# Moving the second part of a modulation weight from SyncE's DMA queue to ACT's in the prologue of a transformer block

## The chip, the cores and the metric

The kernel runs on one core of one Trainium2 chip. The metric is the device time in microseconds (us), the median of several executions of the whole program. One execution of each kernel is profiled; its trace has a span, from the first to the last instruction, some 1.8 us shorter than the device time.

## The reference, cut to what matters

The block is attention with 32 query heads over cached keys and values, followed by a gated MLP with a spatial matmul. Both halves are preceded by a layer norm whose result is scaled and shifted by values computed from a small vector c:

```python
mod = (_silu(c) @ w_mod).reshape(c.shape[0], 6, 1, -1)
sa, ca, ga, sb, cb, gb = (mod[:, 0], mod[:, 1], ...)      # cut
h = _layernorm(x, axis=-1) * (1 + ca) + sa
x = x + ga * _A_ref(h, A_k_cache, A_v_cache, A_wq, A_wo)
```

w_mod is 512 x 3072 in bf16. Only its first two column blocks of 512 (for sa and ca) are needed before the first queries can be projected. The kernel calls them part 0 and part 1, of 512 KB each.

## The kernel before

The order in which loads are issued (cuts marked with ...):

```python
nc.scalar.dma_start(out=c_bf[:], in_=c_dram)
nc.scalar.dma_start(out=x_sb[:, 0, :], in_=x_dram[:, 0, :])
for i in range(2):
    part = slice(i * D, (i + 1) * D)
    nc.sync.dma_start(out=wmod_a[:, :, part], in_=wmod_dram[:, :, part])
...
wqs[0] = early.tile([P, NDT, REP * DH], BF16, name="wq_g")
for dts in (slice(0, 2), slice(2, 4)):
    nc.sync.dma_start(out=wqs[0][:, dts, :], in_=wq_dram[:, dts, 0 : REP * DH])
load_k_nat(0)
nc.sync.dma_start(out=x_sb[:, 1, :], in_=x_dram[:, 1, :])
load_k_nat(1)
...   # further x tiles, the rest of the keys, values, output weights
```

What TensorE does with them. warm(n) issues n matmuls on zeros whose result nobody reads; they bridge the time until data is there and keep the clock up:

```python
xns0 = ln1_norm(0, 1, ln1_stats(0, 1))     # x tile 0, on DVE and GpSimd
mc_ps = bank("misc")
warm(10)
mod_part(0, wmod_a, 0, mc_ps)              # 16 small matmuls, need part 0: "product 1"
warm(6)
mod_part(1, wmod_a, D, mc_ps)              # 16 small matmuls, need part 1: "product 2"
...                                        # transposes of xn, modc, hT, query projection,
                                           # then scores (PE) and exponentials (ACT)
```

## Time and profile before

| | before |
|---|---|
| device time, median (3 runs) | 1321.19 us |
| device time, median (6 runs: these 3 and 3 more, beside the changed kernel) | 1321.04 us (1320.58 to 1321.67) |
| span of the profiled execution (its device time was 1321.45 us, 0.4 above the median) | 1319.7 us |
| product 1 starts, product 2 starts | 5.42, 7.81 us |
| first exponential of the attention starts (ACT) | 11.49 us |

The lines that carry the argument stand in the prediction below. Two more are used: how the loads are issued, and when the first exponential starts. They are from the timelines of SyncE and of ACT; the columns are start in us, duration in us, engine, source line, operation, tiles and count.

```profile
0.73 1.36 SPq L701 DMA_DIRECT2D wmod_a<-in_w_mod_dram  x2
2.13 1.13 SPq L746 DMA_DIRECT2D wq_g<-in_A_wq_dram  x2
11.49 5.61 ACT L980 ACTIVATE pT<-s_ps 128x1024 bf16<-128x1024 f32 x6 [0.68 <-PE s_ps L973]
```

SPq is SyncE's issuing: both parts of the modulation weight first, then the query weights wq_g (512 KB in two halves). The third line begins the attention. From there TensorE and ACT run as a chain to the end.

### The profile page before, as it was taken

The page shows a single profiled execution, that of the slowest core. Times are in us where ns is not written, and L with a number is a line of the kernel's source. Part 1 is how long each engine was busy: PE and PEld are TensorE (multiplying, and loading weights), DVE is VectorE, ACT ScalarE, POOL GpSimd, SP SyncE. Part 2 cuts the span into 40 slices and gives each one's busy share as a digit, 9 for nine tenths or more (in the row PEclk, how much of TensorE's full clock was granted, in tenths as well). Part 3 has the DMA queues.
Part 4 walks back from the last instruction along what each step waited for, and adds up shares of the span by engine and source line. Part 5 has one row for each costly group of instructions (what it writes and reads, how often), then busy time and mean ns, then how long its engine had stood idle before and what let it go on. Part 6 is the DMA issues. An engine that isn't in the chain of part 4 may idle for free.

```text
span 1319.7 us, 27930 instructions
## 1 busy us (share of the span) xinstructions
PE 1312.4 (99%) x12359; PEld 858.6 (65%) x12359; DVE 470.7 (36%) x1162; ACT 1077.1 (82%) x1061; POOL 51.4 (4%) x96
## 2 busy tenths in 40 slices
PE   9999999999999999999999999999999999999998
PEld 5666666666666666666666666666666666644445
DVE  5622222222222222222222222222222566794444
ACT  7899999999999999999999999999999999650000
POOL 1201000000000000000000000000000000020000
PEclk9999999999999999999999999999999999999999
DMA  6542121112101111211110211121111112144300
GB/s 180 146 99 46 21 45 37 37 17 50 37 17 37 30 37 37 33 33 38 33 38 13 53 38 33 17 53 22 33 13 21 25 31 32 34 114 81 70 20 26
DMA packets 148944, 58.64 MB, mean 44 GB/s; under 512 B 138480, under 2 KB 144880, under 8 KB 148816
## 3 DMA queue, kind: packets, MB, share of 16 engines
q1 hardware_dynamic: 141792, 37.65, 15.4%
q0 software_dynamic: 4432, 16.91, 4.5%
q10 hardware_dynamic: 2592, 2.23, 0.5%
q8 instruction: 98, 1.61, 0.5%
q14 instruction: 30, 0.25, 0.1%
HBM read 21.89 MB, written 2.10 MB: 18 GB/s over the span
## 4 chain that ended last, share of the span: by engine, by line
PE 99%; DVE 0%; ACT 0%; issue 0%; DVEq 0%
PE o_ps L995 35%; PE s_ps L973 33%; PE misc L1027 8%; PE misc L940 8%; PE misc L1336 7%; PE s_ps L1182 2%; PE s_ps L1221 2%; PE o_ps L1357 1%; PE o_ps L781 1%; PE s_ps L1357 1%; PE misc L850 0%; DVE hT L809 0%; PE misc L1344 0%; ACT pT L980 0%; DVE tmp L1369 0%; DVE yout L1370 0%
## 5 line engine op out<-in xcount | busy, mean ns | idle before, releaser
L980 ACT ACTIVATE pT<-s_ps 128x1024 bf16<-128x1024 f32 x1024 | 1043.8, 1024 | 82.0 <-PE s_ps L973 6.7
L995 PEld LDWEIGHTS <-pT 128*128 128x128 bf16 x8192 | 548.5, 98 | 241.2
L995 PE MATMUL o_ps<-v,pT 128*128 128x129 bf16 x8192 | 631.5, 220 | 0.0
L973 PE MATMUL s_ps<-qT,kT 128*128 128x512 bf16 x2048 | 608.9, 379 | 0.3 <-ACT pT L980 0.2
L1006 DVE RECIPROCAL rall<-o_ps 128x2 f32<-128x2 f32 x256 | 43.5, 170 | 744.5 <-PE o_ps L995 741.1
L973 PEld LDWEIGHTS <-kT 128*128 128x128 bf16 x2048 | 199.3, 98 | 119.2 <-issue 0.8
L1027 PE MATMUL misc<-wo_g,oT 128*128 128x512 bf16 x512 | 194.1, 379 | 0.0
L940 PE MATMUL misc<-hT,wq_g 128*128 128x512 bf16 (+2 forms) x528 | 190.7, 371 | 0.1
L1007 DVE TENSOR_TENSOR onorm<-o_ps,rall 128x256 bf16<-128x256 f32 x256 | 108.6, 424 | 8.8
L1336 PE MATMUL misc<-wsp,z 128*128 128x512 bf16 (+2 forms) x560 | 100.7, 336 | 0.0
L951 DVE CAST qT<-misc 128x512 bf16<-128x512 f32 x127 | 86.2, 679 | 2.0 <-PE misc L940 2.0
L1336 PEld LDWEIGHTS <-z 128*128 128x128 bf16 x560 | 50.6, 98 | 48.5
L1040 DVE TENSOR_TENSOR xacc<-misc,xacc 128x512 f32<-128x512 f32 x112 | 76.0, 678 | 0.0
L940 PEld LDWEIGHTS <-wq_g 128*128 128x128 bf16 x528 | 50.4, 98 | 1.2 <-issue 0.4
L1027 PEld LDWEIGHTS <-oT 128*128 128x128 bf16 x512 | 50.1, 98 | 0.8
L1351 DVE TENSOR_TENSOR gb<-misc,bsp_bc 128x512 bf16<-128x512 f32 (+1 forms) x28 | 18.4, 658 | 58.9 <-PE misc L1336 58.9
L1182 PE MATMUL s_ps<-win_sb,hT 128*128 128x448 bf16 x128 | 27.0, 352 | 0.0
L1192 ACT ACTIVATE z<-s_ps 128x896 bf16<-128x896 f32 x16 | 14.7, 917 | 14.9 <-PE s_ps L1182 14.9
L1221 PE MATMUL s_ps<-hT,win_sb 128*128 128x512 bf16 x112 | 24.5, 379 | 0.0
L1229 ACT ACTIVATE z1T<-s_ps 128x1024 bf16<-128x1024 f32 x14 | 14.3, 1023 | 10.1 <-PE s_ps L1221 9.1
L692 DVE BATCH_NORM_STATS2 bnst<-x_sb 128x6 f32<-128x512 bf16 x32 | 21.8, 683 | 1.3 <-DMA x_sb<-in_A_x_dram 0.8
L1357 PE MATMUL o_ps<-wout_sb,yT 128*128 128x512 bf16 x84 | 20.1, 379 | 0.0
(88 smaller groups left out, 269.6 us busy)
## 6 DMA issues: line engine op xcount, KB each, us to landing
wq_g<-in_A_wq_dram POOLq DMA_DIRECT2D x7, 512.0 KB, 3.8
v<-in_A_v_cache_dram POOLq DMA_DIRECT2D x7, 512.0 KB, 6.0
wo_g<-in_A_wo_dram POOLq DMA_DIRECT2D x7, 512.0 KB, 4.7
oT<-onorm SPq DMA_TRANSPOSE x128, 2.4
wsp<-in_w_mod_dram POOLq DMA_DIRECT2D x1, 2048.0 KB, 9.0
out_dram<-yout ACTq DMA_DIRECT2D x16, 128.0 KB, 1.7
win_sb<-in_B_w_in_dram POOLq DMA_DIRECT2D x1, 1792.0 KB, 7.8
x_sb<-in_A_x_dram SPq DMA_DIRECT2D x3, 512.0 KB, 5.6
```

The costliest lines, as they stand in the source:

```text
L940: nc.tensor.matmul(ps[0][:, o0 : o0 + n], lhsT=wqs[g][:, dt, hh * DH : (hh + 1) * DH], rhs=hTs[ch][:, dt, c0 : c0 + n], start=(dt == 0), s ...
L951: nc.vector.tensor_copy(out=dst, in_=src)
L973: nc.tensor.matmul(s_ps[:, h * 512 : (h + 1) * 512].rearrange("p (r q) -> p r q", r=REP), lhsT=groups[g]["kT"][:, kt * P : (kt + 1) * P], ...
L980: nc.scalar.activation(out=pTs[u][:, 2 * i : 2 * i + 2, :], in_=s_ps[:].rearrange("p (k q) -> p k q", k=2), func=ACT.Exp, scale=inv_sqrt_dh,)
L995: nc.tensor.matmul(o_ps[:, hh % 2, 0 : DH + 1], lhsT=pTs[u][:, kt, hh * P : (hh + 1) * P], rhs=groups[g]["v1"][:, kt, 0 : DH + 1], start=( ...
L1007: nc.vector.tensor_tensor(out=onorms[u][:, hh - 1 : hh + 1, :], in0=o_ps[:, :, 0:DH], in1=rall[:, c0 : c0 + 2].unsqueeze(2).to_broadcast([ ...
L1027: nc.tensor.matmul(X_ps[:], lhsT=oTs[u][:, hh, :], rhs=groups[g]["wo"][:, hh, :], start=(hh == 0), stop=(hh == REP - 1),)
L1040: nc.vector.tensor_tensor(out=xaccs[j][:], in0=X_ps[:], in1=xaccs[j][:], op=ALU.add)
L1182: nc.tensor.matmul(ps[0][:, hf * 512 : hf * 512 + FC], lhsT=h2Ts[j // CT][:, dt, (j % CT) * P : (j % CT + 1) * P], rhs=win_sb[:, dt, FH + ...
L1221: nc.tensor.matmul(ps[0][:, k * 512 : (k + 1) * 512], lhsT=win_sb[:, dt, f * P : (f + 1) * P], rhs=h2Ts[2 * ch2 + k][:, dt, :], start=(dt ...
L1336: nc.tensor.matmul(g_ps[:, :n], lhsT=z2[:, st, f * P : (f + 1) * P], rhs=wsp[t][:, st, c0 : c0 + n], start=(st == 0), stop=(st == NT - 1 a ...
L1357: nc.tensor.matmul(dst, lhsT=yT[:, f, jj * P : (jj + 1) * P], rhs=wout_sb[:, f, :], start=(f == 0), stop=(f == NFT - 1),)
```

## The change

The intent: take one issue off SyncE, bring part 1 in by the queue that is idle after x tile 0, and let the query weights come right behind part 0.

```diff
     for i in range(2):
         part = slice(i * D, (i + 1) * D)
-        nc.sync.dma_start(out=wmod_a[:, :, part], in_=wmod_dram[:, :, part])
+        (nc.sync, nc.scalar)[i].dma_start(
+            out=wmod_a[:, :, part], in_=wmod_dram[:, :, part]
+        )
```

Nothing else is edited.

## The prediction

> **What bounds the kernel now.** I read the page first, then the chain of waits, then the first 12 us of the timeline, and last the DMA queues in short windows. The page says that TensorE (PE) is the bound from end to end: it is busy in every slice, and the chain that ended last runs over it.
>
> ```profile
> span 1319.7 us, 27930 instructions
> PE 1312.4 (99%) x12359; PEld 858.6 (65%) x12359; DVE 470.7 (36%) x1162; ACT 1077.1 (82%) x1061; POOL 51.4 (4%) x96
> PE 99%; DVE 0%; ACT 0%; issue 0%; DVEq 0%
> ```
>
> The three loads that the change touches are all issued in the first 4 us, and what they feed is over by 10.3 us. So at most 10 of 1320 us (0.8%) are in play at all, and a verdict outside 2% is out of reach by arithmetic. What remains is how far the start shifts, because what follows is a chain without slack: a later start is a later end by the same amount. The chain in order of time, cut to the prologue:
>
> ```profile
> 1.18 4.45 PE o_ps L781 x10
> 5.62 0.41 PE misc L850 x16
> 6.03 1.95 PE o_ps L781 x6
> 7.98 0.39 PE misc L850 x16
> ...
> 8.39 0.16 DVE modc L860
> 8.55 0.08 DVE modc L861
> ...
> 8.73 0.35 DVE hT L809
> ```
>
> L781 are warm-up matmuls whose result nobody reads. L850 are the two modulation products: the first 16 need part 0 of the modulation weight, the second 16 part 1. After them come the modulation columns, hT, the query projection and the first scores. No DMA stands in this chain, but one is just under it. In the list of waits, PE's only wait for a load before 11 us is this:
>
> ```profile
> PEld L850 <- DMA wmod_a<-in_w_mod_dram: 0.5, 1, 0.5
> ```
>
> and the timeline shows that it costs almost nothing today:
>
> ```profile
> 4.14 1.49 PE L781 MATMUL o_ps<-onorm 128*128 128x512 bf16 x3
> 5.24 0.70 PEld L850 LDWEIGHTS <-wmod_a 128*128 128x128 bf16 x16 [0.52 <-DMA wmod_a<-in_w_mod_dram]
> 5.42 0.61 PE L850 MATMUL misc<-sc_bf,wmod_a 128*128 128x1 bf16 x16
> 7.60 0.66 PEld L850 LDWEIGHTS <-wmod_a 128*128 128x128 bf16 x16
> ```
>
> The weight-load side waited 0.52 us, until part 0 landed at 5.24; but the tenth warm-up matmul still streamed. The warm-ups start every 0.43 us from 1.18, so the tenth starts near 5.03 and streams until about 5.45, and the first product starts at 5.42. Part 0 lands exactly when PE becomes free: its slack is nil, and each delay of it is a delay of PE. Part 1 has slack: issued at 1.47 and landed 5.6 us later, near 7.1, against 7.60 where PE takes it.
>
> **What the Trainium skill says.** "DMA: Bandwidth & Descriptors", section "Issuing engines are not separate DMA queues", says that loads issued from SyncE and ACT run on the same 16 engines and interleave, and that a second issuer only saves sequencer time. The same page, section "Queues, rings and completion order", says that SyncE and ACT own one queue row each, and that each DMA engine goes round-robin between the rows with work, packet by packet. The trace agrees: between 3.6 and 3.8 us, while ACT's queue carried x tile 0 and SyncE's carried part 0, the windows show 34 packets of the one and 30 of the other. "TensorE: Matmul & The Clock Gate", section "Part 1: The HAM clock gate", says that PE runs at half rate until it was busy through a free-running window of some 3.4 us. The trace shows warm-up matmuls 0.43 us apart until about 7.17 and some 0.22 apart from there, so the release came about 6.0 us after the first matmul. "ScalarE: Activation LUTs", section "What ACT_TABLE_LOAD costs", gives some 1283 ns; this trace has 1.28 us.
>
> **Part 1: SyncE loses one issue.** The two issues took 1.36 us together, 0.61 to 0.70 each. Everything behind on SyncE is issued some 0.65 us earlier: the query weights at about 1.45 and not 2.13. That gains nothing, since from about 3.6 us on the DMA engines are full and the order of bytes decides. The query weights, issued at 2.13 and 2.83 and 5.7 us in landing, are there at 7.8 and 8.5; their first weight load is at 8.65, behind hT, and its wait is on "issue" and not on a DMA. With the bytes ahead of them doubled up with part 1, they land at about the same time. The key tiles behind them follow the same total of bytes. Value: 0.
>
> **Part 2: ACT gets one issue, 0.6 to 0.7 us.** Its issues end at 1.59 now, the table load runs from 1.62 to 2.90, the exponential from 2.91, and the last small operation of that string (sc_bf on DVE) ends at 3.93. All of it shifts by 0.65 to about 4.6. DVE's next work is at 4.69 (the statistics of x tile 0), and PE needs sc_bf at 5.42. It fits. Value: 0, with 0.1 us to spare on DVE and over a microsecond behind that before xn (ready at 7.03, used at 8.22).
>
> **Part 3: part 1 now competes with part 0.** In one queue part 1 waited behind part 0. In ACT's queue it stands only behind x tile 0, which finishes first. The queue counts from the start of the span, to 4.4, 4.8 and 6.2 us:
>
> ```profile
> q1 hardware_dynamic: 415, 0.42, 29.8%
> q10 hardware_dynamic: 288, 0.13, 12.0%
> ...
> q1 hardware_dynamic: 575, 0.57, 36.9%
> ...
> q1 hardware_dynamic: 1061, 1.06, 51.4%
> ```
>
> q10 is ACT's queue; it stands at its final 288 packets by 4.4 (the same short windows put the last x packets at 4.3). A part is 512 packets of 1 KB and 16 small ones at the end: 528. The windows give q1 351 at 4.2, 494 at 4.6 and 575 at 4.8, so part 0 is through at 4.6 + 0.2 x 34/81 = 4.68, and landed 0.55 later. With part 1 ready in q10 from 4.3 on, q1 gets about half of some 78 packets per 0.2 us: its remaining 528 - 351 = 177 packets from 4.2 on take 177/39 x 0.2 = 0.91 us, until 5.11. Delay of part 0: 5.11 - 4.68 = 0.43 us; it lands near 5.66, and the first product starts near 5.84.
>
> Behind it the six warm-ups start at 6.31, not 5.89. If the clock is released at 7.17 all the same, two run at 0.427 and four at 0.216: the end of the string is 7.17 + 4 x 0.216 = 8.03, against 7.17 + 3 x 0.216 = 7.82 now. Half of the delay is given back, since filler moves from the slow to the fast clock: +0.21. Part 1 itself gets some 195 packets per us from 4.3: 528/195 = 2.7 us, to 7.0, plus 0.5 to 0.9 of landing as for the parts now: 7.5 to 7.9, against a need at 7.60 + 0.21 = 7.81. That may cost 0 to 0.1 more. **Sum: about +0.3 us** in the plain case.
>
> **The rivals.**
> (a) The intended gain. Loads issued sooner arrive sooner, the prologue shortens by up to 0.5 us, and the end comes at about 1320.7. For it: SyncE's string of issues is long (0.73 to 12.75). Against it: the page shows no wait for the query weights or the keys; part 0 was already first in its queue, so nothing can bring it in sooner. I give it 12%.
> (b) The clock is released one window later. The release at 7.17 would end a window from 3.76, in which the PE streamed 1.69 + 1.28 = 2.97 of 3.41 us; the window before it, with 2.58 of 3.41 us, did not release. With the longer gap it is 1.69 + 0.86 = 2.55, about as much as the window that failed. Then everything up to about 10.6 runs at half clock: the six warm-ups end 1.05 us later, the 16 projection matmuls cost some 0.8 more, transposes and the next two warm-ups 0.4. With what DVE hides, +1.9 us: 1323.1. Against it: the windows are my inference from one release, and their phase may not be fixed. I give it 25%.
> (c) No effect: the engines do not share strictly, part 0 is served nearly first, and the shift is under 0.1 us: 1321.2. I give it 20%.
>
> **Range and chances.** The plain case, 43%, gives 1321.19 + 0.3 = 1321.5; (b) pulls the mean up by 0.25 x 1.6 = 0.4, and (a) down by 0.1. I choose 1321.6. The runs before differ by 0.48 us from one another, as much as the effect, so the lower edge is (a)'s 1320.7, and the upper edge just (b)'s, 1323.1. The 2% bounds are 26 us away; only a foreign disturbance would reach them: 0.3% on either side.
>
> **What would show it right or wrong.** Right, if the profile after shows the weight load of the first product waiting for part 0 about 0.9 us, until some 5.6, the product at about 5.8, half of q1's and half of q10's packets between 4.4 and 5.1, the second product at about 8.0, and modc about 0.2 to 0.4 later than 8.39, with the same difference in all later stages. Rival (b) shows as warm-ups still 0.43 us apart past 7.2. Part 2 is wrong if sc_bf ends after 4.7, or if PE waits for it. Part 1 is wrong if any query weight or key product comes to wait for a DMA, or starts earlier relative to modc. The prediction is wrong altogether if part 0 lands before 5.2, or if the span moves by more than the time of modc does.

## The result, and the profile after

The changed kernel takes 1322.57 us (six runs: 1324.83, 1323.30, 1322.60, 1322.54, 1322.47, 1322.38) against 1321.04 us. The ratio is 1.0015, with an interval of 1.0002 to 1.0028. The fastest changed run lies above the slowest run before: some 1.5 us were lost. Here and below a ratio is the mean time of one kernel's runs over that of the other's of the same rounds, so it is not quite the ratio of the medians that are quoted.

The page of the profile after has a longer span and a new entry in the chain of waits, a DMA. (The page counts 206 fewer matmuls on PE than before; those records are missing, and part of the fall in busy time is that.)

```profile
span 1323.0 us, 27724 instructions
PE 1301.6 (98%) x12153; PEld 859.3 (65%) x12359; DVE 471.3 (36%) x1162; ACT 1076.9 (81%) x1061; POOL 51.4 (4%) x96
PE 98%; issue 1%; DMA 1%; DVE 0%; ACT 0%; ACTq 0%; DVEq 0%
```

The timeline of the prologue after the change, by start time, with the idle time before an instruction and what ended it in brackets:

```profile
1.48 1.11 SPq L748 DMA_DIRECT2D wq_g<-in_A_wq_dram  x2
1.64 0.62 ACTq L701 DMA_DIRECT2D wmod_a<-in_w_mod_dram  x1
5.35 0.47 PEld L852 LDWEIGHTS <-wmod_a 128*128 128x128 bf16 x16 [0.87 <-DMA wmod_a<-in_w_mod_dram]
5.77 1.46 PE L783 MATMUL o_ps<-onorm 128*128 128x512 bf16 x6
9.66 0.47 PEld L852 LDWEIGHTS <-wmod_a 128*128 128x128 bf16 x16 [2.94 <-DMA wmod_a<-in_w_mod_dram]
14.81 5.61 ACT L982 ACTIVATE pT<-s_ps 128x1024 bf16<-128x1024 f32 x6 [1.11 <-PE s_ps L975]
```

Product 1 (first L852 line) starts 0.07 us sooner than before, although part 0 landed 0.11 us later. The six warm-ups (L783) are over at 7.23, and then the weight loads stand still until 9.66, when part 1 lands. That wait replaces the filler. The first exponential starts at 14.81 and not at 11.49: 3.32 us later, and the span is 3.3 us longer. So the whole loss of this execution arises before 15 us and is passed on undiminished.

Of the 3.32 us, 1.86 are the later start of product 2 (9.67 against 7.81). The other 1.46 arise between product 2 and the exponential. The chains of waits show them. Before:

```profile
9.40 0.11 PE s_ps L914 x2
9.51 0.11 PE misc L914 x2
```

After, the same query projection:

```profile
1.64 7.98 DMA wmod_a<-in_w_mod_dram
9.67 0.56 PE misc L852 x16
...
11.37 0.21 PE s_ps L916 x2
11.58 0.21 PE misc L916 x2
```

Pairs of 128-column matmuls take 0.21 us and not 0.11: TensorE runs at half clock here. The drop followed its long stand, but not at once: the transposes at 10.08 to 10.25 still start 0.05 to 0.06 us apart, which is the full clock. The other five executions probably had no such drop, or a shorter one: the profiled one is the slowest of the six (1324.83), and they are 1.5 to 2.5 us faster. No profile of them is kept.

### The profile page after: what moved, and what is told of

Same layout as the page of the kernel before. It is cut to its first block, busy times and chain, and to the rows that moved or that the text cites. A ratio compares the mean times of both kernels' runs of the same rounds, so it can differ in the third digit from the quotient of the medians.

```text
span 1323.0 us, 27724 instructions
## 1 busy us (share of the span) xinstructions
PE 1301.6 (98%) x12153; PEld 859.3 (65%) x12359; DVE 471.3 (36%) x1162; ACT 1076.9 (81%) x1061; POOL 51.4 (4%) x96
## 4 chain that ended last, share of the span: by engine, by line
PE 98%; issue 1%; DMA 1%; DVE 0%; ACT 0%; ACTq 0%; DVEq 0%
PE s_ps L975 36%; PE o_ps L997 35%; PE misc L1338 7%; PE misc L942 7%; PE misc L1029 6%; PE s_ps L1184 2%; PE s_ps L1223 2%; PE o_ps L1359 1%; DMA wmod_a<-in_w_mod_dram 1%; PE s_ps L1359 0%; PE misc L852 0%; DVE hT L811 0%; PE o_ps L783 0%; PE misc L1346 0%; ACT pT L982 0%
## 5 line engine op out<-in xcount | busy, mean ns | idle before, releaser
L942 PE MATMUL misc<-hT,wq_g 128*128 128x512 bf16 (+2 forms) x465 | 167.3, 370 | 0.2
L1029 PE MATMUL misc<-wo_g,oT 128*128 128x512 bf16 x386 | 146.3, 379 | 0.0
L718 POOL DMA_DIRECT2D wq_g<-in_A_wq_dram x7 | 5.2, 750 | 370.5 <-PE misc L942 370.5
```

What stands on the lines that cost most here:

```text
L942: nc.tensor.matmul(ps[0][:, o0 : o0 + n], lhsT=wqs[g][:, dt, hh * DH : (hh + 1) * DH], rhs=hTs[ch][:, dt, c0 : c0 + n], start=(dt == 0), s ...
L1029: nc.tensor.matmul(X_ps[:], lhsT=oTs[u][:, hh, :], rhs=groups[g]["wo"][:, hh, :], start=(hh == 0), stop=(hh == REP - 1),)
```

## The experiments

All results were correct, and each kernel was timed beside the kernel before on the same chip. "Landing" is when the load's semaphore is complete, worked out as issue time plus the profile's time to landing; it is 7.1 us for part 1 in the kernel before.

### The changed kernel again (after_again)

No edit.

> The changed kernel once more, for a second profile of it: the first one was of its longest execution (1324.83 us) while the other five lay at 1322.4 to 1323.3. My theory (late part 1): part 1 of the modulation weight lands at 8.5 to 9.6 us instead of 7.1 and TensorE waits for it 1 to 2.5 us; where the wait is long enough the clock drops back to half and adds about 1.5 us more. Expected 1322.5 us, the second product starting between 8.6 and 9.7 us. Rival (clock only): the 1.5 us come from the clock being released later, then the second product starts near 8.0 us and the matmuls before it are 0.43 us apart up to 10 us.

Measured: 1322.69 us (1324.44, 1322.84, 1322.69, 1322.65, 1322.65) against 1321.02; ratio 1.0012, interval 0.9999 to 1.0026. The chain of waits:

```profile
1.64 7.61 DMA wmod_a<-in_w_mod_dram
9.29 0.57 PE misc L852 x16
```

Part 1 landed at 9.25, in the expected band, and the rival (a later release of the clock alone) is out for this execution: PE waits for the load. Again the profiled execution is the one near 1324.5, again with a projection at half clock; the other four agree within 0.2 us at 1322.7. So the common loss is some 1.6 us, and the dropped clock is an extra that the profiled execution showed both times. That the 1.6 us are the wait itself is inferred: no profile of these four is kept. Why it was the profiled one both times is not settled; an execution that stands out as much came in wq_on_act below (1324.59), and there it was not the profiled one.

### The order alone, all on SyncE (order_alone)

```diff
-    for i in range(2): nc.sync.dma_start(wmod_a part i)
+    nc.sync.dma_start(wmod_a part 0)
     nc.sync.dma_start(wq, first half); nc.sync.dma_start(wq, second half)
+    nc.sync.dma_start(wmod_a part 1)
```

> Everything on SyncE as before the change, but part 1 behind the query weights: the order of the change without ACT's queue. If only the bytes ahead of part 1 matter, it lands as late as here as in the changed kernel or later: 512 KB more ahead of it at 350 GB/s are 1.5 us, so about 8.5 us, and the time is 1.0 to 1.5 us above the kernel before (1322.0 to 1322.5). If the lateness comes from ACT's queue (late start at 5.2 us, then a slow tail), this one lands a microsecond earlier than the changed kernel's 9.6 and the time is about 0.7 to 1.2 us above the kernel before.

Measured: 1322.64 us (1322.27 to 1322.87) against 1321.02; ratio 1.0011, interval 0.9997 to 1.0024. The chain:

```profile
2.63 6.45 DMA wmod_a<-in_w_mod_dram
9.13 0.57 PE misc L849 x16
```

Without ACT's queue the loss is the same 1.6 us. (The interval holds 1, as many here do; but the five runs all lie above the nine of the kernel before, whose highest is 1321.31.) Part 1 landed at 9.08, later than the 8.5 us that the bytes ahead would give, though 0.2 to 0.5 us earlier than in the two changed profiles. PE waited 1.10 us for it, and the projection ran at full clock. Letting the query weights pass is therefore enough to make the loss. (Here all 512 KB of them pass, and part 1 is issued at 2.63 us; in the changed kernel only their first half, 256 KB, is issued before part 1.) What it does not show is whether the second queue costs something of its own.

### SyncE held back (sync_held)

```diff
+    nc.vector.memset(wqs[0][:, 0, 0:2], 0.0)    # on DVE, right after sc_bf is made
     nc.sync.dma_start(wq, first half)           # must wait for the memset; all of SyncE's rest follows
```

> The changed kernel, but SyncE issues the query weights and all behind them only after DVE has made sc_bf (about 4.6 us): part 1 stays on ACT's queue behind x tile 0, and nothing is issued beside it. Theory A (what SyncE issues just before and beside it delays it): part 1's first packets come right behind x tile 0 at 4.4 us, it lands at about 6.3 us, and the time is that of the kernel before within 0.5 us (1320.7 to 1321.5). Theory B (a third load on ACT's queue starts late whatever SyncE does): first packets at 5.2 us again, landing near 7.2 us, time again near the kernel before. In both the keys and query weights must still come in time; if they do not, PE waits for a DMA after modc and the time is up to 2 us longer.

Measured: 1320.97 us (1320.88 to 1321.43) against 1321.02; ratio 0.9999, interval 0.9985 to 1.0013. Part 1 is on ACT's queue as in the changed kernel, yet the loss is gone. Product 2 starts behind the filler again:

```profile
6.03 1.84 PE o_ps L784 x6
7.87 0.39 PE misc L853 x16
```

Part 1's first packets came at about 4.5 us, right behind x tile 0, and it landed at 7.3, a microsecond later than theory A said (its last packets ran beside the query weights from 6.0 on). Theory A holds in the start and in the time; B is out. The query weights, issued at 4.7, still came in time, which shows that bringing them forward had nothing to gain.

### More filler (more_warm)

```diff
-    warm(6)
+    warm(16)
```

> The changed kernel with 16 instead of 6 warm-up matmuls between the two modulation products: TensorE does not stand still while part 1 is under way. Part 1 lands as late as before. If the drop of the clock in that wait is a part of the loss, the longest runs (1323.3, 1324.8 us) vanish and the time is 1321.9 to 1322.5 us. If part 1 mostly lands at 8.5 us or earlier, the extra warm-ups (2.2 us at full clock, 4.3 at half) cost more than they give: 1322.5 to 1323.5 us.

Measured: 1323.19 us (1322.70 to 1323.63) against 1321.02; ratio 1.0015, interval 1.0002 to 1.0029. The loads are those of the changed kernel, but part 1 landed at 8.64 this time: landings of the same loads differ by a microsecond between executions (8.64, 9.25, 9.62). The 16 warm-ups ended after it and product 2 started at 9.55. The projection ran at full clock, and no run reached 1324. That agrees with the dropped clock being a consequence of standing still, but the filler cost no less than it saved (1323.19 against 1322.57 and 1322.69 without it), so as a remedy it fails.

### SyncE held back only briefly (sync_held_short)

As sync_held, but the memset follows c_f, so that the query weights are issued at 2.74 us, after part 1 (1.63 to 2.25) and not before it.

> The changed kernel, but SyncE issues the query weights only after DVE has made c_f (about 2.7 us instead of 1.48): after ACT has issued part 1 (1.64 to 2.26), not before it. This parts two causes that the run with SyncE held to 4.6 us left together. Theory A1 (what was issued first is served first, also across the two queues): part 1's first packets come right behind x tile 0 at about 4.5 us, not at 5.2, the query weights come behind it, and part 1 lands near 7.3 us; the time is that of the kernel before within 0.5 us (1320.7 to 1321.5). Theory A2 (the engines share evenly between the queues whatever was issued first): part 1 starts at 4.5 but gets half of the packets from 4.7 on, lands at 8.0 to 8.8 us, and the time is 0.6 to 1.3 us above the kernel before.

Measured: 1321.55 us (1321.31 to 1321.65) against 1321.17; ratio 1.0002, interval 0.9987 to 1.0017. The chain:

```profile
1.63 6.39 DMA wmod_a<-in_w_mod_dram
8.07 0.57 PE misc L853 x16
```

Putting the issue of the query weights behind that of part 1 takes the loss from some 1.6 to 0.4 us. (What is left is not clear of noise in the times, 1321.31 to 1321.65 against 1320.83 to 1321.43, but the profile shows PE waiting 0.71 us for part 1.) The packets per 0.4 us on SyncE's queue / ACT's queue, from the view of the DMA queues, show how (part 1 is in SyncE's queue in "before" and in wq_on_act, and in ACT's in the other two):

| us | before | after | sync_held_short | wq_on_act |
|---|---|---|---|---|
| 4.4 to 4.8 | 160 / 0 | 156 / 1 | 104 / 42 | 157 / 3 |
| 4.8 to 5.2 | 132 / 0 | 114 / 0 | 9 / 124 | 128 / 20 |
| 5.2 to 5.6 | 135 / 0 | 84 / 39 | 0 / 139 | 103 / 46 |
| 5.6 to 6.0 | 145 / 0 | 39 / 88 | 14 / 128 | 70 / 69 |
| 6.0 to 6.4 | 144 / 0 | 30 / 109 | 67 / 49 | 68 / 66 |
| 6.4 to 6.8 | 120 / 0 | 47 / 102 | 87 / 18 | 73 / 57 |
| 6.8 to 7.2 | 157 / 0 | 74 / 82 | 121 / 18 | 89 / 66 |
| 7.2 to 7.6 | 157 / 0 | 94 / 62 | 143 / 12 | 79 / 79 |
| 7.6 to 8.0 | 162 / 0 | 137 / 26 | 162 / 1 | 74 / 78 |

In the changed kernel ACT's queue has nothing of part 1 between 4.4 and 5.2, while SyncE's moves the end of part 0 and then query weights; issued after part 1, they let it start at 4.5 and run almost alone until 6.0 (A1). But its last packets share with what follows, and it lands at 8.02 (A2's band). So the start follows the order of issue across the queues here, and the end is shared. Neither theory was wholly right.

### Part 1 ahead of x tile 0 on ACT (part1_first_on_act)

```diff
+    nc.scalar.dma_start(wmod_a part 1)
     nc.scalar.dma_start(x tile 0)
-    nc.scalar.dma_start(wmod_a part 1)
```

> The changed kernel with ACT's two loads swapped: part 1 is issued at 1.15 us, before SyncE's query weights, and x tile 0 behind it at about 1.8. If the order of issue decides across the queues (theory A1), part 1 starts near 3 us, beside part 0; part 0 then lands 0.3 to 0.6 us later than 5.24 (this is the competition that the prediction reckoned with), part 1 lands before 7.5, and x tile 0, issued behind the query weights' first half, comes 1.5 to 3 us late (statistics start at 6.2 to 7.7 us instead of 4.7), so TensorE waits for xn: 1321.5 to 1323 us. If ACT's queue is slow for any 512 KB load, part 1 still lands after 8.5 us.

Measured: 1324.41 us (1323.19 to 1326.49) against 1321.17; ratio 1.0025, interval 1.0010 to 1.0041. Part 1 landed at 7.06, but x tile 0 came 3.2 us late, and the chain runs over it:

```profile
1.83 6.08 DMA x_sb<-in_A_x_dram
7.91 0.02 issue
7.93 0.71 DVE bnst L692
```

ACT's queue is thus not slow for a 512 KB load. The competition with part 0 that the prediction and this expectation reckoned with came late: part 1's first packets came at 4.0 us, when 428 of part 0's 528 packets were through. From there the two shared (82 packets to 72 until 4.4), but x tile 0 had not shared with part 0 before, and part 0 was there for product 1 at 5.10, the earliest of all runs.

Not the whole loss is x tile 0's. Against the kernel before, the first transpose starts 2.11 us later (10.33 against 8.22) and the first exponential 3.34 us: the rest arose at half clock, as in the two changed profiles (pairs of the projection 0.21 us apart).

### x tile 0 on SyncE between the parts (x0_on_sync)

Only c remains on ACT's queue; SyncE issues part 0, x tile 0, part 1.

> The kernel before with x tile 0 on SyncE between the two parts, so that ACT's queue carries only c. Part 0 no longer shares with x tile 0 (128 KB, 0.35 us at 350 GB/s): it lands at 4.7 to 4.9 us instead of 5.24, x tile 0 near 5.3, part 1 as before near 7.1. With ten warm-ups ending near 5.45 TensorE cannot use it: 1320.8 to 1321.4 us, the same as before. If the low DMA rate between 3.0 and 3.6 us (some 100 packets in 0.6 us) comes from the second queue's start, it is gone here and part 1 lands by up to 0.5 us earlier.

Measured: 1322.25 us (1321.82 to 1322.66) against 1321.17; ratio 1.0007, interval 0.9993 to 1.0020. The expectation failed: part 0 came at 5.13, part 1 landed at 8.47, and PE waited for it. The low rate at 3.2 to 3.6 us was gone (127 packets against 58 on both queues before), but between 4.4 and 6.0 us the queue moved only 91 to 114 packets per 0.4 us, against 132 to 160 before. Why is open; the run shows that one queue alone is not better.

### Less filler in the kernel before (fewer_warm)

```diff
-    warm(6)
+    warm(4)
```

> The kernel before with 4 instead of 6 warm-ups between the products, to see how much room there was ahead of the wait that the change created. Part 1 lands near 7.1 us and the second product could start at 7.3 instead of 7.8: up to 0.4 us shorter, 1320.6 us. If less warm-up puts off the release of the clock, 0.5 to 1.5 us longer: 1321.5 to 1322.5.

Measured: 1320.93 us (1320.71 to 1321.25) against 1321.17; ratio 0.9999, interval 0.9985 to 1.0012. The profiled execution was 0.8 us shorter in span, the medians differ by 0.24 us, and the interval holds 1. (The profile of the kernel before is of an execution 0.4 us above its median.) The room ahead of the wait is a few tenths of a microsecond at most.

### The query weights on ACT's queue (wq_on_act)

Both parts on SyncE as before; the two halves of the query weights behind x tile 0 on ACT.

> The mirror of the change: both parts stay on SyncE (0.73 and 1.47 us), and the query weights go onto ACT's queue behind x tile 0 (about 1.64 us). Two queues are used as in the changed kernel, but the order of issue is that of the kernel before. Theory A1 (order of issue decides): part 1 lands at 7.0 to 7.6 us and the time is within 0.4 us of the kernel before (1320.8 to 1321.5). Theory C (whatever is split over two queues comes late): part 1 lands after 8 us and the time is 1321.8 us or more.

Measured: 1322.16 us (1321.69, 1321.79, 1322.16, 1322.41, 1324.59) against 1321.00; ratio 1.0013, interval 0.9999 to 1.0026. All five lie above the nine of the kernel before, whose highest is 1321.60. Theory A1 alone is wrong; the time is in theory C's range, the landing just under it. The chain of the profiled execution, the 1321.69 one:

```profile
1.48 6.45 DMA wmod_a<-in_w_mod_dram
7.97 0.57 PE misc L850 x16
```

The last column of the table has the reason: with part 1 in one queue and the query weights in the other, the two run side by side at nearly equal packet counts from 5.6 to 8.0, and part 1 lands at 7.92, PE waiting 0.80 us for it. Splitting these loads over two queues was thus a cost of its own, though part 1 had been issued first. Its size is not sure: the profiled execution is the fastest of the five and shows 0.17 us by the start of the first exponential, while the medians differ by 1.16. The order is also not quite that of the kernel before, for the first key tile was issued (2.13) before the second half of the query weights.

### A try at a better version (before_held_fewer)

The kernel before, with the query weights and all behind them held until sc_bf (issued at 3.99) and warm(4).

> A try at a better version: the kernel before with everything behind the two parts on SyncE issued only after sc_bf (about 4 us), and 4 warm-ups between the products. Nothing queued behind part 1 can slow its last packets, so it should land at 6.5 to 6.9 us instead of 7.1, and the second product starts at about 7.1: 1320.3 to 1320.9 us. If the query weights or keys then come too late, TensorE waits for a DMA after modc and it is 1321 us or more.

Measured: 1320.98 us (1320.80 to 1321.30) against 1321.00; ratio 1.0, interval 0.9986 to 1.0013. Part 1 landed at 7.12 all the same, not at 6.5 to 6.9: in one queue, what stands behind it was not slowing it. No version beats the kernel before.

### Query weights ahead, the rest held (rest_held)

The changed kernel, with the keys and all behind them on SyncE issued at 4.65, after sc_bf.

> The changed kernel with the query weights issued at 1.48 us as there, ahead of part 1, but all that follows on SyncE (keys, further x tiles, values) held until sc_bf, about 4.6 us. This parts the late start of part 1 from its slow end. If the query weights issued ahead are the whole cause, part 1 starts at 5.2 us as in the changed kernel and lands about as late (9 us or more), and the time is 1322.3 us or more. If the loads that follow beside it make the slow end, part 1 still starts near 5.2 but has the engines nearly alone once the query weights are through (512 + 512 KB from 4.7 us at 350 GB/s end near 7.7): it lands near 8.2 us, and the time is 0.5 to 0.8 us above the kernel before (1321.6 to 1321.9).

Measured: 1322.35 us (1322.14 to 1322.82) against 1321.29; ratio 1.0008, interval 0.9994 to 1.0022. The chain:

```profile
1.63 7.04 DMA wmod_a<-in_w_mod_dram
8.71 0.57 PE misc L853 x16
```

Part 1 began at 5.2 again and landed at 8.67; the loss is 1.06 us by medians, against 1.6. So the query weights issued ahead make about two thirds of the loss, and the loads that follow beside it perhaps a third. The split is rough: it rests on medians of two sessions, and the landing of the same loads without the hold ranged from 8.64 to 9.62.

### The meter over all profiles

The shift of the first exponential against the kernel before, beside the shift of the span, each from one profile: after +3.32 and +3.3; after_again +2.85 and +2.9; part1_first_on_act +3.34 and +3.4; more_warm +1.74 and +1.8; order_alone +1.33 and +1.2; rest_held +0.91 and +0.9; sync_held_short +0.36 and +0.2; wq_on_act +0.17 and +0.2; sync_held -0.11 and -0.1; before_held_fewer -0.54 and -0.5; fewer_warm -0.68 and -0.8. Only x0_on_sync is off (+0.75 and +1.2). What the prologue loses is lost at the end. These shifts read some 0.4 us smaller than differences of medians, because the profile of the kernel before is of an execution that much above its median.

The profiles can also be sorted by how long TensorE stood before the projection. After 2.44 us (after) and the two stands shown first below, the projection ran at half clock; after the third, and after 1.14 (rest_held) and 1.10 us (order_alone), it ran at full clock:

```profile
10.33 0.23 PE L889 MATMUL misc<-ident,xn 128*128 128x128 bf16 x1 [2.72 <-DVE xn L681]
9.29 0.55 PE L852 MATMUL misc<-sc_bf,wmod_a 128*128 128x1 bf16 x16 [1.59 <-DMA wmod_a<-in_w_mod_dram]
8.52 0.55 PE L851 MATMUL misc<-sc_bf,wmod_a 128*128 128x1 bf16 x16 [1.25 <-DMA wmod_a<-in_w_mod_dram]
```

They are from part1_first_on_act, after_again and x0_on_sync. With more_warm, which filled the stand, this speaks for the stand as the cause of the drop. It is one profile of each program, so no limit between 1.25 and 1.59 us is shown.

## Why the prediction was right or wrong

The bound was read right: PE end to end, at most 10 us in play, shifts of the start passed on one for one. The last was shown in all profiles but one. That the measured 1322.57 us lies within the range is luck: the upper edge, 1323.1, was that of rival (b), which did not happen as told, and the plain case reached only 1321.5. The size was not right: +0.4 us was forecast and +1.5 us came, for a reason that stood in the sum with at most 0.1 us. (The mean is also a little off its own terms: 1321.5 + 0.4 - 0.1, less 0.06 for rival (c), is 1321.7 and not 1321.6.)

- **Part 1 of the change (SyncE's earlier issues gain nothing): right.** sync_held issues the query weights more than 3 us later than the changed kernel and loses nothing. But "value: 0" looked only for a gain. What the earlier query weights cost part 1, on the other queue, has no term in the sum.
- **Part 2 (ACT's later string fits): right.** sc_bf ended at 4.61, foretold as about 4.6, and PE did not wait for it.
- **Part 3, part 0 delayed by 0.43 us: wrong.** The step assumed that part 1 would have packets ready from 4.3 us and take half. In the changed kernel its first packet came at about 5.2, after part 0 was through. Part 0 landed 0.11 us later in the first profile and 0.49 us later in the second (5.73), neither with part 1's packets beside it. In part1_first_on_act the two did share from 4.0, but x tile 0 had not been beside part 0, which was earliest there. So the halving of a shift by faster filler, built on this step, did not come to bear.
- **Part 3, part 1 landing at 7.5 to 7.9 against a need at 7.81: the step that failed.** It was 9.62 and 9.25. The arithmetic, half of the packets from 4.3 on, missed two things. The start is 0.9 us later, because the first half of the query weights had been issued 0.16 us ahead of it on the other queue (the delay is gone in sync_held and sync_held_short); this alone moves the landing from 7.5 to 7.9 us to 8.4 to 8.8 (an estimate: the 0.9 us added). And the last packets trickle beside what SyncE has queued: 26 in the 0.4 us from 7.6, 12 in those from 8.0. The rate between was forecast well: 482 of the 528 packets went from 5.2 to 7.6, 200 per us where the sum had 195. In place of "0 to 0.1 more", and of 0.3 us in all, product 2 came 1.86 us later in the profiled execution; the medians of after_again put the whole loss at some 1.6 us.
- **Rival (b), the clock, in the form told: wrong.** It foresaw slow warm-ups past 7.2 us. In the profile after, the ten warm-ups took 3.79 and not 4.45 us: the release came at about 4.2 us and not at 7.17. The fixed windows read out of one release were not fixed. But a clock effect did come, of 1.46 us, in another place: a drop after the wait for part 1, in the profiled execution.
- **Rivals (a) and (c): wrong**; nothing was gained, and no effect would have been 1321.2. Of (c), one half came close: part 0 was served nearly first, and landed 0.11 us later in the first profile.

Of the prediction's signs of being right, one ("the weight load of the first product waiting for part 0 about 0.9 us") was met almost to the digit, 0.87 us, although the mechanism behind it was not there: the wait began earlier, because the faster clock ended the warm-ups sooner. A number that fits is not yet a cause shown. The other signs failed: the queues had 156 and 1 packets between 4.4 and 4.8 and not half each, the second product started at 9.67 and not near 8.0, and modc came 1.87 us later (10.26 against 8.39) and not 0.2 to 0.4. By its own last test the prediction was wrong altogether in this execution: the span moved by 3.3 us, more than modc did, and the difference is the dropped clock.

What stays open: what decides when a load's first packet goes when both queues have work (x tile 0, 128 KB, started 1.7 us after its issue, when a fifth of part 0's packets were through, while part 1 in its place waited 2.8 us); why landings of the same loads differ by a microsecond; why the dropped clock showed in the profiled executions of the changed kernel; and what the 1324.59 us execution of wq_on_act did, which has no profile.

## What to carry to other kernels

When several loads are in flight at once, ask for each not only "in what queue" but "how many bytes go before it or beside it until its last packet", and issue the one with the least slack first, on whichever queue, before its rivals. Moving a load to an idle queue was not free here, and letting a load with slack (the query weights, which could be issued 3 us later at no loss) pass one without slack cost the full wait. In a chain without slack, as this one, such a microsecond reaches the end whole, however small it is against the total.

## What the Trainium skill lacked or had wrong

- "DMA: Bandwidth & Descriptors", sections "Queues, rings and completion order" and "Issuing engines are not separate DMA queues": the round-robin between queue rows agrees with wq_on_act once both run (70 and 69 packets in 0.4 us), but an even split was not the rule: in the changed kernel ACT's queue got 88 and 109 packets against SyncE's 39 and 30 from 5.6 to 6.4, with both loads unfinished. The page does not say which of two loads in different queues starts first. Here part 1 on ACT's queue had its first packet 3.6 us after its issue (5.2 us) when 256 KB had been issued on SyncE 0.16 us ahead of it, and at 4.5 us when they were issued after it. That issuing from several engines only saves sequencer time is not all of it: nearly the same order of loads, split over two queues, cost 1.16 us by medians (wq_on_act).
- "TensorE: Matmul & The Clock Gate", Part 1: the release is not at a fixed time, as the page says; the profiles have it between 4 and 7.2 us for the same ten warm-ups. The page's section "Why this matters for your kernels" names idle gaps above some 3 us as what drops the clock; here it had dropped after PE stood still 2.72 (part1_first_on_act), 2.44 (after) and 1.59 us (after_again), and had not after 1.25 us (x0_on_sync).
